# Block sums of the last units and of the first token group moved from GpSimd to VectorE, and a later place for one small product

## The chip, the core and the metric

The kernel runs on one core of a Trainium2 chip. The metric is the time of one execution on the device, in microseconds (us), as the median of several runs. The engines are called as in the profile: PE is TensorE (PEld its weight loads), DVE is VectorE, ACT is ScalarE, POOL is GpSimd, SP is the engine that issues most transfers.

## What is computed

```python
# x: 8 x 3008 x 256, filters: 1505 x 256, all float32 or float64 on input
X = np.fft.rfft(x, axis=1)
Y = X * (filt_r + 1j * filt_i)[None]
y = np.fft.irfft(Y, n=3008, axis=1)            # 8 x 3008 x 256
x2 = y.reshape(24064, 256)
h = x2 @ w_in                                  # 256 -> 2048
g = h - np.tanh(h)
out = g @ w_out                                # 2048 -> 256
```

## The kernel before

**Two halves.** The Fourier part is done as matrix products in steps (`first`, `middle`, `last`) over five batches of sequences called `UNITS` (one, two, two, two, one sequence). The second half, the two large products with the function h - tanh(h) between them, starts as soon as the first batch of sequences has its frequencies back, and the Fourier steps of the later batches are spread between its instructions.

**Token groups and units.** The tokens are cut into 48 groups of up to 512 (the last one has 448). For every group, the 2048 hidden features are cut into four quarters. A group and a quarter together are a *unit* (a word that the code also uses, as `U`, from 0 to 191; it has nothing to do with `UNITS`). The work on a unit goes through three steps: `up` makes h with products on PE, `shrink` turns h into g with arctan and squares on ACT and multiplications on DVE, and `down` multiplies g by `w_out` and accumulates in PSUM. A loop runs `U` from 0 to 193; in each round it interleaves `up(U)`, `shrink(U - 1)` and `down(U - 2)` by hand, as Python generators that are advanced with `next`. Nothing reorders what this loop issues: each engine carries out its own instructions in this order, and waits by semaphores for what it needs. In the last two rounds (`U` of 192 and 193) there is no `up` any more, and a short loop with `k` from 0 to 4 advances `shrink` twice and `down` twice at each `k`.

**Seven products instead of eight.** Both large products are done on blocks of 2 by 2 with seven block products instead of eight (a Strassen scheme). It needs four sums of the blocks of the input beforehand and some sums of the products afterwards. The sums of the input blocks are made by `combine(b, t)`, which issues four subtractions into `t[0]` to `t[3]`; `t[1]` needs `t[0]`, and `t[3]` needs `t[1]`.

- For the first large product the sums are those of the group's tokens. They are made at the end of `last(i)`, into the tile `tu`, from the tile `ut`, 128 x 256 elements each. `up` uses them in its products named x and z (lines L545).
- For the second large product the sums are those of g, and are made at the end of `shrink(U)`, right after `end(0)` (L633, the last multiplication of `shrink`, done in place in the tile `h`), into the tile `t`, 128 x 2 x 256 elements each (128 x 2 x 224 in the last group). `down` uses them: products 1, 2 and 3 read `h` itself, product 5 reads `t[0]`, product 6 `t[1]`, product 7 `t[2]`, product 4 `t[3]` (L680). They are issued in the order (1, 2), (3, 5), (6, 7), (4).

In the kernel before, the four subtractions (L524 to L527) are all on POOL. The one exception is the third of the very last unit, which is on DVE. The weights need the same kind of sums; those are on POOL too (`sums`, L260 to L263), and are made in the first stretch, as the weights come in.

**Around the opening.** The first group's `last(0)` is issued in full before the loop. Then `up(0)` begins: products x and y on `ut`, a copy `s` on ACT, a step of the conversion of late weights on DVE (L204, L205, L207), the sum of h on DVE that reads the bank of y (L571), the product x on `tu`, and then a product `pf` of the next batch's Fourier step, whose PSUM bank is that of y.

**Around the end.** After the last unit's products, `down(191)` adds them up (L693 to L713, on ACT, DVE and POOL), transposes the result on PE (L756), copies it from PSUM (L758, L760) and stores it (L767). Between these, `bounded` decides whether all |h| were below a bound: a comparison of the sums of squares `y_sums` (L781), a minimum over them (L783), a product of that column with a column of ones on PE, `pc` (L785), which adds up the 128 partitions, and a conversion into the integer `count` (L786). The program ends by reading `count`, and goes through a slower general kernel (`general`) if the bound did not hold. With the inputs at hand it holds.

Of the kernel before, what the change touches and what calls it, by code (L numbers as in the profile page):

```python
# [143 lines left out]
def kernel(  # L144
# [162 lines left out]
    def weights_slow(tiles, quarters):  # L307

        jobs = parts_of(quarters)
        began = [begun(tiles, job, True) for job in jobs[:2]]  # L310
        yield
        for k in range(len(jobs)):
            for _ in began[k]:
                yield
            if k + 2 < len(jobs):
                began.append(begun(tiles, jobs[k + 2], True))
            if k % 2:
                sums(quarters[k // 2])
                yield
# [180 lines left out]
    def last(i, z):  # L500


        p, c = groups[i]
        ws_ = widths(p, c)
        n = sum(ws_)
        e2 = e2s.pop(i)
        ut = dn.tile([128, 2, CH * 128], F32, tag="ut", bufs=2, name="ut")
        for h in range(2):
            pu = z("pu", [128, CH * 128])
            for j, w in enumerate(ws_):  # L510
                nc.tensor.matmul(pu[:, j * 128:j * 128 + w], e2[0:w, j, h * 128:(h + 1) * 128],  # L511
                                 s2[0:w, 0:w], start=True, stop=True)
            ACT.copy(ut[:, h, 0:n], pu[:, 0:n])
            if h == 0:
                yield
        w = n // 2
        tu = dn.tile([128, 4, 256], F32, tag="tu", bufs=2, name="tu")
        b = [[ut[:, h, k * w:(k + 1) * w] for k in range(2)] for h in range(2)]
        combine(b, [tu[:, k, 0:w] for k in range(4)])
        uts[i] = (b, tu, w)  # L520
        yield

    def combine(b, t, shared=False):
        G.tensor_sub(t[0], b[0][1], b[0][0])  # L524
        G.tensor_sub(t[1], b[1][1], t[0])  # L525
        (V if shared else G).tensor_sub(t[2], b[1][1], b[0][1])  # L526
        G.tensor_sub(t[3], t[1], b[1][0])  # L527


    hs, gs = {}, {}  # L530
# [76 lines left out]
    def shrink(U):  # L607

        h, w = hs.pop(U)
        ht = {k: h[:, k:k + 2].rearrange("p a b n -> p (a b) n")[:, :, 0:w] for k in (0, 2)}  # L610

        def tiles(tag, bufs):
            return dn.tile([128, 4, 256], F32, tag=tag, bufs=bufs, name=tag)[:, :, 0:w]

        y, sq = {}, {}

        def turn(k):
            y[k] = tiles("y", 2)
            ACT.activation(y[k], ht[k], AF.Arctan, scale=S)  # L619

        def power(k):
            ACT.activation(y[k], y[k], AF.Square,  # L622
                           accum_out=y_sums[:, 2 * U + k // 2:2 * U + k // 2 + 1])

        def times(k):
            V.tensor_mul(ht[k], ht[k], y[k])  # L626

        def square(k):
            sq[k] = tiles("sq", 1)
            ACT.activation(sq[k], y[k], AF.Square, bias=near_b, scale=A)  # L630

        def end(k):
            V.scalar_tensor_tensor(out=ht[k], in0=sq[k], scalar=K, in1=ht[k],  # L633
                                   op0=ALU.add, op1=ALU.mult)


        turn(2)
        power(2)
        yield
        times(2)  # L640
        yield
        square(2)
        turn(0)
        yield
        end(2)
        yield
        power(0)
        times(0)
        square(0)
        yield  # L650
        end(0)
        t = dn.tile([128, 4, 2, 256], F32, tag="t", bufs=2, name="t")
        blocks = [[h[:, 2 * a + k, :, 0:w] for k in range(2)] for a in range(2)]
        combine(blocks, [t[:, k, :, 0:w] for k in range(4)], U + 1 == 4 * len(groups))
        gs[U] = (blocks, t, w)
        yield

# [115 lines left out]
            nc.sync.dma_start(dst, src)  # L773
        del outs[:n]

    def bounded(z):


        small = tr.tile([128, 2 * 4 * len(groups)], F32, tag="a2", bufs=2, name="small")
        least = cst.tile([128, 1], F32, name="least")  # L780
        V.tensor_single_scalar(out=small, in_=y_sums, scalar=float(np.arctan(S * NEAR) ** 2),  # L781
                               op=ALU.is_lt)
        V.tensor_reduce(out=least, in_=small, axis=mybir.AxisListType.X, op=ALU.min)  # L783
        pc = z("pc", [1, 1])
        nc.tensor.matmul(pc, least, ones, start=True, stop=True)  # L785
        V.tensor_copy(count, pc)  # L786

    def general(sb, ps):

# [66 lines left out]
    with tc.tile_pool(name="tr", bufs=2) as tr, tc.manual_schedule():  # L856
        with tc.tile_pool(name="pro", bufs=1) as pro, \
# [136 lines left out]
            for j in range(NK // 2):  # L994
# [7 lines left out]
                for i in range(2):  # L1002
                    k = (2 * j + i) % 4
# [34 lines left out]
        with tc.tile_pool(name="dn", bufs=2) as dn, \  # L1038
# [22 lines left out]
            def filters_d():  # L1061
# [15 lines left out]
                for v, row, m, i, n, src in filter_rows(0, NK):  # L1077
                    G.dma_start(dram(filt_d, ((row * 2 + v) * NK + i) * DM,
                                     [[2 * NK * DM, m], [DM, n], [1, DM]]), src)
                    yield  # L1080

            late, copies = weights_slow(tiles1, range(7, 8)), filters_d()
            total = 4 * len(groups)
            for _ in last(0, z1):
# [2 lines left out]
            for U in range(total + 2):  # L1087
                i, u = divmod(U, 4)
                if U < total:
                    p, c = groups[i]  # L1090
                    if c == 0 and u == 0:
                        units = 4 * len(CHUNKS[p])
                        steps, done = [], 0 if p else EARLY
                        if p + 1 < len(UNITS):
                            n_f = len(chunks_of(UNITS[p + 1], XH))
                            n_m = 2 * NK // (3 - len(UNITS[p + 1]))
                            steps = [0.01 * units + 1.36 * units * (k - done) / (n_f - done)
                                     for k in range(n_f)]
                            lo, hi = 1.6 * units, 5 * units - 17
                            steps += [lo + (hi - lo) * k / n_m for k in range(n_m)]  # L1100
                            ms = None
                    if u == 0 and i + 1 < len(groups) and c + 1 < len(CHUNKS[p]):
                        e2s[i + 1] = load_e2(*groups[i + 1])
                    if u == 2 and i + 1 < len(groups) and c + 1 == len(CHUNKS[p]):
                        assert done == len(steps)
                        e2s[i + 1] = load_e2(*groups[i + 1])
                    if u == 0 and c + 1 == len(CHUNKS[p]) and p + 2 < len(UNITS):
                        fs = first(p + 2, z1)
                        next(fs)
                    if u == 2 and i + 1 < len(groups):  # L1110
                        lasts = last(i + 1, z1)
                sh = shrink(U - 1) if 0 <= U - 1 < total else iter(())
                dw = down(U - 2) if 0 <= U - 2 < total else iter(())

                def d():

                    next(dw, None)

                def e():

                    next(dw, None)

                def s():

                    next(sh, None)

                def t(k):


                    nonlocal ms, done  # L1130
                    quarter[0] = k
                    if k == 2 and stores:
                        store(*stores.pop())
                    store_some(4)
                    if U >= total:
                        return
                    pos = 20 * c + 5 * u + k
                    if u == 3 and k in (0, 2) and i + 1 < len(groups):
                        next(lasts)
                    elif done < len(steps) and steps[done] <= pos:  # L1140
                        if done < n_f:
                            next(fs)
                        else:
                            next(ms)
                        done += 1
                        if done == n_f:
                            ms = middle(p + 1, z1)
                            next(ms)
                    next(late, None)
                    if U > 0 and k in (1, 3):  # L1150
                        next(copies, None)

                if U < total:
                    if U == total - 1:
                        one = tr.tile([128, 128], F32, tag="x", bufs=3, name="one_sb")
                        nc.sync.dma_start(one, one_d)
                        ones = cst.tile([128, 1], F32, name="ones")
                        G.memset(ones, 1.0)
                    up(U, d, e, s, t)
                else:  # L1160
                    for k in range(5):
                        s()
                        s()
                        d()
                        e()
                        t(k)
                        if U == total + 1 and k == 0:
                            bounded(z1)
            for w in stores:
                store(*w)  # L1170
            store_some(len(outs))
# [36 lines left out]
```

## Time and profile before

| | |
|---|---|
| median of 6 runs | 2805.44 us (2802.91 to 2807.14) |
| the profiled execution's own time | 2805.67 us |
| span of its instructions | 2803.9 us |
| busy share of the span: PE, PEld, DVE, ACT, POOL | 97%, 81%, 68%, 67%, 63% |
| mean granted TensorE clock | 0.991 |

The span is the time from the first to the last instruction in the profile. A line of a timeline gives start, length, engine, source line, operation, the tile written and the tiles read, with the shapes, a count of instructions merged into the line and, in brackets, the idle time of that engine before it with what ended it. A line of the chain of work that ended last gives start, length and what. A row of a table by windows gives the window, its length, the busy time of PE, PEld, DVE, ACT and POOL with the count of instructions, the granted TensorE clock as a share, the busy share of the transfer engines, and GB/s.

### The profile page before, as it was taken

What the parts mean: (1) busy time and instruction counts of PE and PEld (TensorE: products, weight loads), DVE (VectorE), ACT (ScalarE), POOL (GpSimd) and SP (SyncE); (2) the same over time, 40 slices, a digit from 0 to 9 for tenths busy, and PEclk for the clock granted to TensorE, in tenths of its full rate; (3) what the DMA queues carried; (4) which work ended last, traced back from release to release, by engine and by line L of the source; (5) the groups of instructions that cost most, each with busy time, mean ns of one, the idle gap of its engine ahead of it and who ended that gap; (6) DMA issues with size and microseconds to landing.
All of it is one profiled execution on the core that took longest, in us unless ns stands there. A gap on an engine that the chain in (4) does not pass through costs nothing.

```text
span 2803.9 us, 36463 instructions
## 1 busy us (share of the span) xinstructions
PE 2718.8 (97%) x12438; PEld 2272.7 (81%) x12438; DVE 1910.4 (68%) x2175; ACT 1886.4 (67%) x2790; POOL 1768.9 (63%) x1407
## 2 busy tenths in 40 slices
PE   4899999999999999999999999999999999999998
PEld 2577778888888888888888888888888888898887
DVE  6755666666776777665677776766676676677776
ACT  2476777666767776666677777666666666666665
POOL 5546887544776777544576777654476667555655
PEclk7999999999999999999999999999999999999999
DMA  9854442322333222223323233112223222111010
GB/s 248 214 185 123 105 126 75 90 83 72 79 78 77 69 72 59 64 78 88 82 70 75 71 81 82 38 45 64 59 67 86 55 58 62 25 20 25 16 22 17
DMA packets 322591, 217.53 MB, mean 78 GB/s; under 512 B 224782, under 2 KB 274746, under 8 KB 322156
## 3 DMA queue, kind: packets, MB, share of 16 engines
q1 hardware_dynamic: 266826, 157.28, 23.6%
q10 hardware_dynamic: 52818, 51.53, 6.0%
q0 software_dynamic: 2752, 6.30, 0.9%
q8 instruction: 100, 1.64, 0.2%
q14 instruction: 95, 0.78, 0.1%
HBM read 138.87 MB, written 79.17 MB: 78 GB/s over the span
## 4 chain that ended last, share of the span: by engine, by line
PE 82%; DVE 6%; ACT 4%; issue 2%; POOL 2%; DMA 2%; SPq 1%; ACTq 0%; DVEq 0%; POOLq 0%
PE o L680 34%; PE x L545 20%; PE z L545 10%; PE y L545 5%; PE pe L411 3%; PE pz L430 3%; PE pu L511 3%; PE pf L351 2%; DVE h L626 2%; ACT y L622 1%; DVE h L596 1%; DMA raw<-in_moe_w_in_dram 1%; ACT y L619 1%; DVE h L633 1%; SPq L773 0%
## 5 line engine op out<-in xcount | busy, mean ns | idle before, releaser
L626 DVE TENSOR_TENSOR h<-h,y 128x1024 f32<-128x1024 f32 (+2 forms) x384 | 575.8, 1500 | 312.3 <-ACT y L622 310.8
L680 PE MATMUL o<-t,wd 128*128 128x256 f32 (+2 forms) x3072 | 776.5, 375 | 1.8 <-POOL t L526 1.3
L680 PEld LDWEIGHTS o<-t,wd 128*128 128x128 f32 x3072 | 580.5, 190 | 93.9 <-issue 22.0
L633 DVE SCALAR_TENSOR_TENSOR h<-sq,h 128x1024 f32<-128x1024 f32 (+2 forms) x384 | 558.8, 1455 | 122.8 <-ACT sq L630 114.8
L524 POOL TENSOR_TENSOR t<-h 128x512 f32<-128x512 f32 (+2 forms) x192 | 240.5, 1253 | 553.0 <-DVE h L633 402.4
L680 PE MATMUL o<-h,wd 128*128 128x256 f32 (+2 forms) x2304 | 582.3, 375 | 4.0 <-DVE h L633 4.0
L545 PE MATMUL x<-tu,wu 128*128 128x256 f32 (+2 forms) x2304 | 582.0, 375 | 4.2 <-POOL tu L525 2.1
L545 PEld LDWEIGHTS x<-tu,wu 128*128 128x128 f32 x2304 | 430.4, 190 | 105.1 <-issue 42.6
L680 PEld LDWEIGHTS o<-h,wd 128*128 128x128 f32 x2304 | 430.1, 190 | 77.4 <-issue 16.0
L630 ACT ACTIVATE sq<-y,near_b 128x1024 f32<-128x1024 f32 (+2 forms) x384 | 435.1, 1133 | 6.5 <-DVE h L633 0.2
L619 ACT ACTIVATE y<-h 128x1024 f32<-128x1024 f32 (+2 forms) x384 | 397.3, 1035 | 14.4 <-ACT e L414 6.4
L622 ACT ACTIVATE y<-y 128x1024 f32<-128x1024 f32 (+2 forms) x384 | 399.9, 1041 | 6.6 <-ACT a L352 0.4
L551 ACT COPY s<-x 128x512 f32<-128x512 f32 (+2 forms) x192 | 110.9, 577 | 327.9 <-PE x L545 309.8
L527 POOL TENSOR_TENSOR t<-t,h 128x512 f32<-128x512 f32 (+2 forms) x192 | 319.0, 1661 | 0.1
L551 ACT COPY u<-x 128x512 f32<-128x512 f32 (+2 forms) x384 | 221.1, 576 | 138.0 <-PE x L545 119.6
L525 POOL TENSOR_TENSOR t<-h,t 128x512 f32<-128x512 f32 (+2 forms) x192 | 246.2, 1282 | 15.1
L526 POOL TENSOR_TENSOR t<-h 128x512 f32<-128x512 f32 (+2 forms) x191 | 245.9, 1287 | 0.0
L446 POOL TENSOR_TENSOR zs<-zs,ft 128x512 f32<-128x512 f32 x112 | 165.2, 1475 | 90.0 <-ACT zs L444 89.9
L447 POOL TENSOR_TENSOR uv<-uv,zs 128x512 f32<-128x512 f32 x112 | 206.8, 1846 | 9.1 <-DVE uv L445 0.5
L545 PE MATMUL x<-ut,wu 128*128 128x256 f32 (+2 forms) x768 | 198.4, 381 | 10.5 <-DVE h L596 8.4
L588 DVE TENSOR_TENSOR h<-z,u 128x512 f32<-128x512 f32 (+2 forms) x192 | 128.8, 671 | 112.1 <-ACT u L551 111.1
L545 PE MATMUL z<-tu,wu 128*128 128x256 f32 (+2 forms) x768 | 194.6, 376 | 0.0
(122 smaller groups left out, 3291.3 us busy)
## 6 DMA issues: line engine op xcount, KB each, us to landing
a<-ct SPq DMA_DIRECT2D x64, 384.0 KB, 3.9
ft<-filt SPq DMA_DIRECT2D x96, 256.0 KB, 4.5
out_dram<-ot SPq DMA_DIRECT2D x1392, 16.0 KB, 1.5
ct<-e ACTq DMA_DIRECT2D x112, 192.0 KB, 2.2
ct<-a ACTq DMA_DIRECT2D x80, 256.0 KB, 2.9
x_sb<-in_x_dram SPq DMA_DIRECT2D x69, 256.0 KB, 2.9
e<-ct SPq DMA_DIRECT2D x33, 512.0 KB, 4.2
fg<-fg SPq DMA_DIRECT2D x40, 392.0 KB, 5.1
```

Of the source, the lines that this page charges most:

```text
L524: G.tensor_sub(t[0], b[0][1], b[0][0])
L525: G.tensor_sub(t[1], b[1][1], t[0])
L526: (V if shared else G).tensor_sub(t[2], b[1][1], b[0][1])
L527: G.tensor_sub(t[3], t[1], b[1][0])
L545: nc.tensor.matmul(bank[:, k], wu[:, q - 1, (2 * u + k) * 128:(2 * u + k + 1) * 128], rhs[q - 1], start=(first and k == 0), stop=True, ski ...
L551: ACT.copy(t, X)
L619: ACT.activation(y[k], ht[k], AF.Arctan, scale=S)
L622: ACT.activation(y[k], y[k], AF.Square, accum_out=y_sums[:, 2 * U + k // 2:2 * U + k // 2 + 1])
L626: V.tensor_mul(ht[k], ht[k], y[k])
L630: ACT.activation(sq[k], y[k], AF.Square, bias=near_b, scale=A)
L633: V.scalar_tensor_tensor(out=ht[k], in0=sq[k], scalar=K, in1=ht[k], op0=ALU.add, op1=ALU.mult)
L680: nc.tensor.matmul(product(q), wd[:, q - 1, (2 * u + k) * 128: (2 * u + k + 1) * 128], rhs[q - 1][:, k], start=(u == 0 and k == 0 and q == ...
```

## The change

`combine` is given the engine for all four subtractions. The sums of `tu` are on DVE for the first group and on POOL for the 47 others. The sums of `t` are on DVE for units 190 and 191 and on POOL for the others. `bounded` becomes a generator with two steps: the comparison and the minimum are issued in the last round at `k` of 0, after the first pair of the last unit's products and before the additions L693 and L694; the product `pc` and the conversion are issued at `k` of 2, after the products (6, 7).

```diff
-        combine(b, [tu[:, k, 0:w] for k in range(4)])
+        combine(b, [tu[:, k, 0:w] for k in range(4)], G if i else V)
...
-    def combine(b, t, shared=False):
-        G.tensor_sub(t[0], b[0][1], b[0][0])
-        G.tensor_sub(t[1], b[1][1], t[0])
-        (V if shared else G).tensor_sub(t[2], b[1][1], b[0][1])
-        G.tensor_sub(t[3], t[1], b[1][0])
+    def combine(b, t, by):
+        by.tensor_sub(t[0], b[0][1], b[0][0])
+        by.tensor_sub(t[1], b[1][1], t[0])
+        by.tensor_sub(t[2], b[1][1], b[0][1])
+        by.tensor_sub(t[3], t[1], b[1][0])
...
-        combine(blocks, [t[:, k, :, 0:w] for k in range(4)], U + 1 == 4 * len(groups))
+        combine(blocks, [t[:, k, :, 0:w] for k in range(4)],
+                G if U + 2 < 4 * len(groups) else V)
...
-    def bounded(z):
+    def bounded():
...
         V.tensor_reduce(out=least, in_=small, axis=mybir.AxisListType.X, op=ALU.min)
-        pc = z("pc", [1, 1])
+        yield
+        pc = z1("pc", [1, 1])
         nc.tensor.matmul(pc, least, ones, start=True, stop=True)
         V.tensor_copy(count, pc)
+        yield
...
+            bound = bounded()
...
                         d()
+                        if U == total + 1 and k in (0, 2):
+                            next(bound)
                         e()
                         t(k)
-                        if U == total + 1 and k == 0:
-                            bounded(z1)
```

As built, the four sums of `tu` of the first group stand on DVE between the conversion passes of earlier weights and L204, that is before L204, L205, L207 and L571. The four sums of unit 190 stand on DVE between L633 of that unit and L604, the last sum of h in unit 191. The four of unit 191 stand behind its last L633; behind them come L781, L783, L694, L700, the conversion to `count` and L705. On PE the order changes only by `pc`, which moves from behind the products (1, 2) to behind (6, 7).

## The prediction

> **What bounds the kernel now.** I read the busy shares first, then the list of who waited for whom on PE, then the chain that ended last, then the instructions around the two edited places.
>
> ```profile
> PE 2718.8 (97%) x12438; PEld 2272.7 (81%) x12438; DVE 1910.4 (68%) x2175; ACT 1886.4 (67%) x2790; POOL 1768.9 (63%) x1407
> ```
>
> The waits, as engine and line, whom it waited for, us in total, times, longest:
>
> ```profile
> PE x L545 <- POOL tu L525: 2.1, 1, 2.1
> PE pc L785 <- DVE least L783: 1.9, 1, 1.9
> ...
> PE o L680 <- POOL t L526: 1.3, 1, 1.3
> ...
> PE o L680 <- POOL t L527: 0.5, 1, 0.5
> ```
>
> PE is the bound, so an edit is worth only the PE idle time it removes, or what it takes off the work after PE's last product. Each of these four waits happens once. The first is in the opening of the first token group, the other three are in the last 30 us. The chain shows how those three follow each other (start, length, what):
>
> ```profile
> 2776.59 1.16 POOL t L524
> ...
> 2777.82 1.86 POOL t L525
> 2779.68 1.94 POOL t L526
> 2781.62 1.95 POOL t L527
> ...
> 2783.61 2.74 PE o L680 x12
> ...
> 2787.68 0.56 DVE least L783
> ...
> 2788.47 4.92 PE o L680 x16
> ```
>
> Unit 190's four sums take 6.97 us on POOL. VectorE works on unit 191 meanwhile, and the two slow each other:
>
> ```profile
> 2775.36 1.08 DVE L633 SCALAR_TENSOR_TENSOR h<-sq,h 128x896 f32<-128x896 f32 x1
> ...
> 2782.67 1.83 DVE L633 SCALAR_TENSOR_TENSOR h<-sq,h 128x896 f32<-128x896 f32 x1
> ...
> 2784.61 0.62 DVE L526 TENSOR_TENSOR t<-h 128x448 f32<-128x448 f32 x1
> ```
>
> The same L633 takes 1.08 us alone and 1.83 beside POOL. One sum costs 0.62 on DVE, 1.14 on POOL undisturbed. After unit 191's first eight product matmuls PE stands still from 2786.34 to 2788.29, because the bound's product is next in its order. Then the clock drops:
>
> ```profile
> 2790.00:2791.00 1.00, 1.00 (x4) 0.93 (x3) 0.02 (x1) 0.35 (x1) 0.00 (x0) 0.50 0.00 0
> ```
>
> The seventh figure, 0.50, is the granted clock. The windows around it (0.84 from 2789 to 2790, 0.96 from 2793 to 2794) put the half clock at about 0.32 + 3 + 0.08 = 3.4 us, costing 1.7 us of PE work.
>
> **Unit 190's sums.** On DVE they stand between L633 (ends 2776.44) and L604, the last sum of h in unit 191. One after another, with 0.03 us before a dependent one, they end at about 2778.9 where POOL ended at 2783.56. PE's 28 product matmuls of unit 190 (0.19 apart) then run without the 1.29 and 0.53 us waits and end near 2782.1. That alone brings nothing: the next product needs unit 191's last L633. Queued behind the sums on DVE are L604, L626, L633, L626, L633. L604 slips from 2776.36 to 2778.8 and ends 2779.4, so ACT's second arctan waits for it (2778.48 before, 2779.45 now). From there: L626 to 2780.4, L633 to 2781.5; the square's ACT pass ends 2781.5 (0.95 + 0.95 + 0.19); L626 to 2782.6, L633 to 2783.8, all at the undisturbed 1.07 to 1.08 us since POOL is silent. PE starts unit 191 at 2783.83 instead of 2784.56: **0.7 us gained**. Beyond those five nothing waits for the sums. No DMA is moved, nor any queue passed.
>
> **Unit 191's sums and the bound.** The sums follow L633 on DVE and end at 2784.4, 2785.0, 2785.6 and 2786.2. The products that read them come 1.5 us (first) and 3.0 us (second and third) after PE's start, that is from 2785.3 and 2786.9, so PE does not wait. The comparison and the reduction (0.53 + 0.56) stand behind the sums on DVE and end near 2787.3, under PE's products, so they cost nothing; without that cover they would cost 1.1. L694 and L700 wait behind them, but nobody needs those before L707. The bound's product now follows the third pair of products at 2788.4 and finds its input ready. Removed: from the end of eight matmuls at 0.19 (2786.07) to the restart at 2788.41, **2.3 us**. New on the path: the bound's two matmuls and the conversion to `count` (0.15) stand before L705 on DVE: **0.2 us lost**.
>
> **The clock.** In the profiled run the 16 matmuls from 2788.41 took 4.98 us; at 0.19 each they take 3.2: **1.8 us**. Whether this goes depends on idle time. The 1.95 us gap was followed by half clock; those of 1.29 and 0.53 were not, nor was PE's longest wait between 200 and 600 us (3.3, for POOL's `uv` near 245: the clock reads 1.00 from 240 to 270). So length alone does not decide; where the gap falls does too. The new gap before unit 191, 2782.06 to 2783.83, is 1.8 us. I take it as mostly not enough, as it is shorter than the two (1.95, and 2.08 in the opening) that did bring half clock. The Trainium skill ("TensorE: Matmul & The Clock Gate", section "Why this matters for your kernels") asks for no PE-idle gaps over about 3 us; this trace drops the clock after 1.95, so the measurement decides. By the page neither gap would drop it, and this term would be nothing.
>
> Tail: 0.7 + 2.3 + 1.8 - 0.2 = **4.6 us**; L705 comes at 2788.8 instead of 2793.42. What follows (L706, L707, L713, the transposes, the two stores) keeps its lengths. If half clock hits unit 191 in the new kernel, 1.7 comes back: 2.9.
>
> **The first group's sums.** They gain nothing, though their wait is the longest of the four.
>
> ```profile
> 122.34 0.79 POOL L261 TENSOR_TENSOR wd<-wd 128x256 f32<-128x256 f32 x1
> ...
> 124.40 0.69 DVE L571 TENSOR_TENSOR h<-y,s 128x512 f32<-128x512 f32 x1 [0.98 <-ACT s L551]
> ...
> 126.29 1.14 PE L545 MATMUL x<-tu,wu 128*128 128x256 f32 x4 [2.08 <-POOL tu L525]
> ...
> 127.25 1.88 PE L351 MATMUL pf<-x_sb,wf_sb 128*128 128x512 f32 x2
> ```
>
> On POOL they stand behind four sums of `wd` (to 124.69). On DVE they start when the first copy of `ut` ends, 122.2 (the transfers they also wait for are those PE's first matmul of the group waited for, which started at 122.22), in front of three conversion passes (L204, L205, L207; 0.42 each) and of L571. The matmul on `tu` can start at 124.05, 2.2 us earlier. But the next one in PE's order, `pf`, writes the bank that L571 reads, and L571 now stands behind seven instructions. Beside POOL's `wd` sums each DVE sum waits for a POOL one: the rows show a blocked DVE instruction ending 0.28 (L205, L207) after its POOL neighbour, and a blocked POOL one of this size 0.6 after its own. Alternating gives 122.6, 123.5, 124.4 and 125.3 for the four, 126.4 after the conversions, L571 to 127.04, `pf` at 127.28 against 127.25: **0.0**. If POOL never got in the way (0.42 each from 122.2), `pf` would be held only to about 126.7: 0.6 gained. If each DVE sum cost a whole POOL instruction (0.8) and its full 0.42, the four end at 127.0 and `pf` comes at 129.0: 1.7 lost. I take 0, nearest to the L205 and L207 rows, which stand beside the very same POOL sums. The Trainium skill ("SBUF — State Buffer", section "Who interferes with whom") speaks against this edit: a VectorE instruction with two SBUF inputs and a GpSimd one reading SBUF exclude each other for the whole instruction. L571, with one input in PSUM, kept its 0.69 beside POOL, as the page says. With the full 0.42 after each block the page would put `pf` some 0.5 us later than my sum.
>
> The opening also ran at half clock for 3.4 us (0.73 from 125 to 130, 0.93 from 130 to 135) behind a 2.08 us idle; the new idle is 125.2 to 127.3, as long. So this stays, unless it falls differently on the clock's accounting: then up to 1.4 us go (133.48 now, 132.05 with the two `pf`, `z` and copies at full clock).
>
> **Sum.** The profiled execution took 2805.67 us, a span of 2803.9 and 1.8 around it, 0.2 above the median 2805.44. 2805.67 - 4.6 = 2801.0. I keep 2801.0 for the median; 0.2 is less than the terms are known to. Of this kernel, a measurement can tell about 0.2% from no change, 5.6 us: below 2799.8 is faster, above 2811.1 slower.
>
> **Rivals.**
> (a) As forecast, and the opening's half clock goes or POOL's `wd` sums hardly block: 0.6 to 2.0 more (both), 2799.0 to 2800.4, half of it past the bound. For it: half clock depends on where the idle falls, and this idle moves. Against: idle as long as before.
> (b) Half clock comes after the new gap before unit 191, or `pf` is held by whole POOL instructions: 1.7 each, 2802.7, both 2804.4.
> (c) Slower: the sums do not run at 0.62 on DVE. Unit 190's four delay unit 191's last L633 fourfold, and the sixth product needs three more. With s for one sum (over 1.0, so that the sums and not PE set the pace), L705 comes at 2783.8 + 4(s - 0.62) + 3s + 2.1, which passes 2793.42 at s = 1.43; at POOL's disturbed 1.95 the end is 3.6 us later, 2809.3. Against it: the 0.62 row is the same shape and operands, even started just before a POOL sum.
> (d) The edits do nothing: excluded, the order of VectorE's and PE's instructions does change as told.
>
> **Numbers.** Forecast 0.52, (a) 0.30, (b) 0.13, (c) 0.05. Half of (a), 0.15, lies past the bound for faster, and a quarter of the forecast, 0.13, since the six times before spread over 4.2 us and its middle is only 1.2 from the bound: 0.28. Slower by more than 0.2% needs 7(s - 1.43) above 5.4, s above 2.2: 0.03. Range 2799.0 to 2804.2: the low end takes in (a), the high end nearly all of (b).
>
> **What would show it.** PE's wait for `least` and both waits for `t` in the last units gone; L526 at 0.62 on DVE eight times over; L633 at 1.08 throughout the tail; a PE gap of about 1.8 us before unit 191's first product; from that product to L705 some 4.9 us, where it was 8.9. In the opening, the matmul on `tu` near 124.1 and `pf` still near 127.3. Wrong if `pf` moves by over a microsecond, if L604 delays unit 191 past 2784.6, or if the bound's product still waits.

## The result, and the profile after

The changed kernel takes 2800.47 us in the median of 17 runs, beside 2805.97 us for the kernel before in 37. The ratio is 0.998, with a 95% interval of 0.9974 to 0.9987: about 5.5 us less, 0.20%, with an interval that leaves out 1. The forecast was 2801.0 us, with a range of 2799.0 to 2804.2. Two later measurements of the same kernel gave 0.9982 and 0.9983. The ratios here and below are those on record; they are estimates of their own, not the quotient of the two medians, and differ from it by up to 0.0003.

The two profiled executions are closer together: 2805.67 and 2802.76 us, 2.9 us apart. From unit 190's last L633 to `pu` they differ by 4.5 us. But the first copy of `ut` ends 1.3 us later in the changed one (122.17 and 123.44); this end lies anywhere from 121.2 to 123.9 in the fourteen profiles of this document. Single executions scatter by more than the terms of the sum, so the terms are read below from distances within a trace.

The page of the changed kernel's profile (span, then busy us, share and instructions) shows eleven instructions fewer on POOL and eleven more on DVE:

```profile
span 2800.9 us, 36459 instructions
...
PE 2717.0 (97%) x12438; PEld 2271.3 (81%) x12438; DVE 1914.9 (68%) x2186; ACT 1886.9 (67%) x2790; POOL 1755.4 (63%) x1396
```

In the list of PE's waits (us in total, times, longest) of the changed kernel, `tu` on POOL, `least` and both waits for `t` are gone. Two others have come or grown:

```profile
PE o L682 <- DVE h L633: 5.8, 9, 1.8
...
PE pf L351 <- DVE h L571: 1.7, 1, 1.7
```

The first is the new gap before unit 191's first product (1.81 us, forecast 1.8). The second is the opening's idle, moved from the product on `tu` to `pf`.

The chain of work that ended last (start, length, what) now runs through DVE in the tail, where it ran through POOL. Source lines moved by two at this place; L705 is now L707.

```profile
2777.64 0.64 DVE t L524
...
2778.30 0.62 DVE t L525
2778.92 0.54 DVE t L526
2779.46 0.53 DVE t L527
2779.99 0.53 DVE h L604
...
2783.89 1.10 DVE h L633
...
2785.04 4.81 PE o L682 x24
...
2790.15 0.31 DVE pu L707
```

Unit 190's four sums take 2.36 us, from 2777.64 to 2780.00, instead of 6.97, L604 waits behind them as forecast, and 24 of unit 191's products run in one piece.

### The profile page after: what moved, and what is told of

Read it like the earlier page. It is cut to its first block, busy times and chain, and to the rows that moved or that the text cites. A ratio compares the mean times of both kernels' runs of the same rounds, so it can differ in the third digit from the quotient of the medians.

```text
span 2800.9 us, 36459 instructions
## 1 busy us (share of the span) xinstructions
PE 2717.0 (97%) x12438; PEld 2271.3 (81%) x12438; DVE 1914.9 (68%) x2186; ACT 1886.9 (67%) x2790; POOL 1755.4 (63%) x1396
## 4 chain that ended last, share of the span: by engine, by line
PE 82%; DVE 6%; ACT 5%; DMA 3%; issue 2%; POOL 2%; ACTq 0%; SPq 0%; DVEq 0%; POOLq 0%
PE o L682 34%; PE x L545 20%; PE z L545 10%; PE y L545 5%; PE pe L411 3%; PE pz L430 3%; PE pu L511 3%; DVE h L626 2%; PE pf L351 2%; ACT y L622 1%; ACT y L619 1%; DVE h L596 1%; DMA raw<-in_moe_w_in_dram 1%; DVE h L633 1%; ACT sq L630 0%
## 5 line engine op out<-in xcount | busy, mean ns | idle before, releaser
L626 DVE TENSOR_TENSOR h<-h,y 128x1024 f32<-128x1024 f32 (+2 forms) x384 | 576.2, 1501 | 311.9 <-ACT y L622 310.8
L633 DVE SCALAR_TENSOR_TENSOR h<-sq,h 128x1024 f32<-128x1024 f32 (+2 forms) x384 | 558.9, 1455 | 122.4 <-ACT sq L630 114.0
```

## The experiments

For every kernel I read four distances from its trace: from the end of the first copy of `ut` to `pf` and to the first product of `down`; from unit 190's last L633 to unit 191's first product and to `pu` (L705 before, L707 after); and the granted clock. "Before" in a row is the kernel before on the same chip.

**Each part alone.** The parts are the three pieces of the change: the sums of `tu`, the sums of `t`, and the place of `bounded`. The cuttings are shortened. In the first run `combine` for `t` and the place of `bounded` are as before; in the second `tu` and `bounded`; in the third both `combine` calls; in the fourth only `tu`.

```diff
 e2, e3, e4:  combine(b, [tu ...], G)                    # first group's sums on POOL
 e1, e3:  combine(blocks, [t ...], as before: POOL, third of unit 191 on V)
 e1, e2:  e(); t(k); if k == 0: next(bound); next(bound)    # bound at its old place
```

> Only the first group's sums of tu are on VectorE; units 190 and 191 and the bound's product are as before. Theory A (the opening gives nothing, all of the gain is made in the tail): the median stays within 0.7 us of before (ratio 1.0000 +- 0.0003), and pf (L351) starts about as long after the end of the first copy of ut as before (5.1 us). Theory B (the opening has a share, since the changed kernel's profile shows pf only 4.7 us after that copy, and no half clock behind it): 1 to 2 us faster (ratio 0.9993 to 0.9996), with PE's wait before pf under 1.8 us and full clock from there on. In the tail PE's waits for t and for least, and the 1.95 us gap, must stand as before.

> Only the eight sums of units 190 and 191 are on VectorE; the bound's comparison, minimum and product follow the first pair of products as before. Theory A (sums and bound are separate terms, 0.7 us for the sums): unit 191's first product starts about 7.4 us after unit 190's last L633 ends (8.1 before); the product pc still holds PE, behind four sums, L694, L781 and L783 on VectorE, for about 2 us, so the gain is 0.6 us and half clock can still follow (ratio about 0.9998). Rival C (the sums were the whole cause, the bound's wait is only there because VectorE was slowed by POOL): PE's wait for least shrinks below 0.5 us and the gain is 3 us or more (0.9989).

> Only the bound is moved: comparison and minimum after the first pair of unit 191's products, pc after (6, 7). All sums are as before, on POOL but for the third of unit 191. Theory A: unit 191's first product starts 8.1 us after unit 190's last L633 as before, PE's wait for least is gone, L705 comes 2.1 us earlier after that product if the clock stays full or half in both, and 3.9 earlier where the half clock goes with the gap: 2.1 to 3.9 us faster (ratio 0.9986 to 0.9993). Rival C: POOL's sums of unit 191 hold PE instead (t[1] and t[3] on POOL come 2.9 and 4.1 us after L633), and the gain is under 1.5 us.

> The whole change except the first group: tu is on POOL for all groups. Theory A (the opening gives nothing): as fast as the changed kernel, 4.5 to 5.5 us faster than before (ratio 0.998). Theory B (the opening has a share of 1 to 2 us): 3.5 to 4.5 us faster (0.9984 to 0.9988), and in the profile PE waits 2.1 us for POOL's tu again. In both the tail must look like the changed kernel's, L705 about 12.5 us after the end of unit 190's last L633.

| kernel | `ut` to `pf`, to first `down` | L633 to unit 191, to `pu` | median, before beside it | ratio, interval |
|---|---|---|---|---|
| before | 5.09, 29.30 | 8.11, 16.98 | | |
| changed | 4.72, 27.44 | 7.43, 12.47 | 2800.47, 2805.97 | 0.998 (0.9974 to 0.9987) |
| e1, opening | 4.72, 27.43 | 8.11, 16.98 | 2806.96, 2807.31 | 0.9998 (0.9989 to 1.0007) |
| e2, sums | 5.50, 29.38 | 7.44, 14.60 | 2806.00, 2807.31 | 0.9992 (0.9983 to 1.0001) |
| e3, bound | 5.55, 29.59 | 8.12, 13.16 | 2804.01, 2807.31 | 0.9985 (0.9976 to 0.9994) |
| e4, sums and bound | 5.16, 27.84 | 7.44, 12.48 | 2802.77, 2807.31 | 0.9984 (0.9975 to 0.9993) |

The medians alone would not separate the parts; the distances do, to a few hundredths of a microsecond. The sums bring 0.67 us (8.11 to 7.44) and leave PE's wait for the bound standing, so rival C (the sums were everything) falls. The timeline of e2 shows that wait, and DVE at its undisturbed speed under it:

```profile
2786.22 0.35 DVE L783 TENSOR_SCALAR small<-y_sums 128x384 f32<-128x384 f32 x1
2786.61 0.55 DVE L785 TENSOR_REDUCE least<-small 128x1 f32<-128x384 f32 x1
2787.31 0.19 PE L788 MATMUL pc<-ones,least 128*1 128x1 f32 x2 [1.93 <-DVE least L785]
...
2788.67 2.81 PE L682 MATMUL o<-t,wd 128*128 128x224 f32 x14
```

The last 14 products take 2.81 us here. In the kernel before they took 4.49 under half clock, behind a gap 0.02 us longer. Moving the bound brings 2.1 us at full clock: `pu` comes 7.16 us after unit 191's first product in e2 and 5.04 in e4, which differ in nothing else in the tail. In e3 POOL's sums of unit 191 are ready in time, so rival C falls there too.

e1 gives half to each of its theories: `pf` at 4.72 and no half clock in the opening, as theory B expected, but a median within 0.4 us of before, as theory A did; half clock came at 246.8 us instead. e4's ratio of 0.9984 lies on the border between its two theories and decides nothing.

**Only unit 190's sums.** e4, with unit 191's sums as before (POOL, the third on VectorE).

> tu on POOL for all groups, the bound moved, unit 190's four sums on VectorE, unit 191's sums as before (POOL, the third on VectorE). Theory A (unit 191's sums are ready in time on either engine; the 0.7 us come from unit 190's): L705 12.5 to 12.8 us after unit 190's last L633, as in e4, and the same median within 0.5 us (ratio 0.9984). Rival C (the sums of the last unit matter, since nothing is left to hide them): PE waits 0.5 to 1.5 us for t of unit 191, L705 at 13.0 to 14.0.

Unit 191 starts 7.43 us after L633 and `pu` comes at 12.47 us, within 0.01 of e4 (2801.86 us, ratio 0.9982, 0.9973 to 0.9992). The four sums of unit 191 on VectorE are worth nothing here; all of the 0.67 us comes from unit 190's.

**A busy POOL.** The changed kernel with six more subtractions on POOL, whose results are not used.

```diff
+        if U + 2 == 4 * len(groups):
+            scr = dn.tile([128, 4, 256], F32, tag="tu", bufs=2, name="scr")
+            for k in range(6):
+                G.tensor_sub(scr[:, 2 * (k % 2):2 * (k % 2) + 2, 0:w], blocks[0][1], blocks[0][0])
```

> The changed kernel with six subtractions that nobody reads put on POOL beside unit 190's sums and unit 191's multiplications; they read SBUF only. It prices the silent POOL that the sum for the tail rests on. Theory A (VectorE instructions with two SBUF inputs take turns with POOL): the sums take 0.95 to 1.8 us instead of 0.62, L626 and L633 1.8 to 2.0 instead of 1.08, L604, with one input in PSUM, stays at 0.61; unit 191's first product 11 to 13.5 us after unit 190's last L633 (7.4 in the changed kernel), so that a tail with the sums on VectorE beside a busy POOL is slower than the tail before (8.1). Rival (POOL is the one that waits): 7.4 to 8.0 us, the sums at 0.62.

The timeline of this kernel:

```profile
2776.46 0.63 DVE L524 TENSOR_TENSOR t<-h 128x448 f32<-128x448 f32 x1
...
2777.12 1.44 DVE L525 TENSOR_TENSOR t<-h,t 128x448 f32<-128x448 f32 x1
...
2781.43 0.61 DVE L604 TENSOR_TENSOR h<-z,u 128x448 f32<-128x448 f32 x1
...
2783.55 1.84 DVE L633 SCALAR_TENSOR_TENSOR h<-sq,h 128x896 f32<-128x896 f32 x1
...
2788.58 4.10 PE L686 MATMUL o<-h,wd 128*128 128x224 f32 x10 [6.00 <-DVE h L633]
```

Sums with two SBUF inputs wait for POOL (1.44, then 1.55 and 1.55; the first, started ahead of POOL, keeps 0.63); L604, with one input in PSUM, does not. L626 and L633 took 1.49, 1.84 and 2.02 us as long as POOL worked, less than expected for the first, and the last L633, after POOL was done, 1.09. Unit 191 starts 12.16 us after L633, inside the expected 11 to 13.5, and `pu` comes 2.3 us later than in the kernel before (half clock fell into both tails). So the sums are cheap on VectorE only because POOL is silent in the tail. This is the mechanism of the prediction's slower rival; the time is that of a single execution, 2807.66 us.

**PE kept busy in the gap.** The kernel before, with work on PE that the result does not need.

```diff
+        fill = z("fill", [128, 2, 128])
+        for _ in range(4):
+            nc.tensor.matmul(fill, wf1[:, 0], wf1, start=True, stop=True)
         pc = z("pc", [1, 1])
```

> The kernel before, with four matmuls of 128x256 that nobody reads put on PE ahead of pc, so that PE works for about 1.7 us of the 1.95 us gap. It adds work that the result does not need. Theory A (the half clock in the tail comes from the gap): never half clock in the tail, L705 7.1 to 7.4 us after unit 191's first product instead of 8.9, so 0.8 to 1.7 us faster on the median, depending on how often the gap brings half clock (ratio 0.9994 to 0.9997). Rival D (the half clock falls there whatever PE does, or the matmuls delay pc): no gain or up to 0.5 us slower.

2804.14 us beside 2805.46 (ratio 0.9995, 0.9986 to 1.0004): inconclusive. In its profile half clock came earlier, from 2786.6 to 2790.0, behind the two waits for POOL's `t` (1.29 and 0.53) that the filler does not cover, and `pu` 8.0 us after unit 191's first product. Theory A's "never half clock" is wrong: those two waits together can bring it (here both lie whole in the 3.41 us ahead of it; the last section says why that matters).

**Other openings.** All three are the changed kernel otherwise. In e7 and e8 the first step of the late conversion is left out at the first unit's first quarter, so that every later step comes a quarter later; in e7 and e9 only `t[0]` and `t[1]` of `tu` are on VectorE; in e9 the step follows L571 within the same quarter. The cuttings are shortened, and one line is in words.

```diff
 e7, e8:  -   next(late, None)
          +   if U or k: next(late, None)
 e7, e9:  t[0], t[1] on V and t[2], t[3] on POOL, for the first group
 e9:      -   t(0)                                   # before L571
          +   if U: t(0)
              d(); shrinks(0)
              V.tensor_add(h[:, 0, :, 0:w], Y, s1)   # L571
          +   if not U: t(0)
```

> The changed kernel with another opening: for the first group only t[0] and t[1] of tu are on VectorE, t[2] and t[3] on POOL, and the first step of the late conversion (L204, L205, L207) comes one quarter later, so that L571 stands right behind t[1]. If what stands in front of L571 holds pf, as the prediction's sum for the opening says, pf starts 3.1 to 3.4 us after the first copy of ut (4.7 in the changed kernel, 5.1 before), and the first down product 1.3 to 1.7 us earlier than in the changed kernel: 1.0 to 1.7 us faster than the changed kernel (ratio to before about 0.9975). If the opening's gains are given back later (half clock that comes behind the wait for uv near 246 us whenever it does not come in the opening), the stretch from the copy of ut to unit 190's last L633 stays within 0.5 us of 2654.2 and the median within 0.7 us of the changed kernel's.

> The changed kernel with the first step of the late conversion one quarter later and all four sums of tu on VectorE. L571 follows the fourth sum: pf 3.9 to 4.1 us after the first copy of ut, 0.7 us earlier than in the changed kernel, where it stands behind three conversions. On the median 0.5 to 0.8 us faster than the changed kernel, or the same if the opening's gains are given back near 246 us.

> The changed kernel with another opening: t[0] and t[1] of the first group's tu on VectorE, t[2] and t[3] on POOL, and L571 ahead of L204, L205 and L207; the late conversion keeps its quarter. If e7 lost its gain only because the conversion came a quarter later and fell on unit 1's L597, this one keeps it: pf 2.9 us after the first copy of ut and the first down product at 25.6 to 26.3 us (27.4 in the changed kernel), 1 to 1.8 us faster than the changed kernel (ratio to it 0.9994 to 0.9996), unless the half clock near 246 us takes it back. If ACT's and VectorE's chain through unit 0 sets the first down product whatever PE does: 27.0 to 27.5, and no gain.

| kernel | `ut` to `pf`, to first `down` | median, changed kernel beside it | ratio to before, interval |
|---|---|---|---|
| changed | 4.72, 27.44 | | |
| e7 | 2.90, 27.45 | 2800.77, 2801.22 | 0.9986 (0.9977 to 0.9995) |
| e8 | 3.71, 28.08 | 2802.36, 2801.22 | 0.9986 (0.9977 to 0.9995) |
| e9 | 2.90, 25.68 | 2798.40, 2802.07 | 0.9973 (0.9962 to 0.9983) |

Expected of the yardsticks:

> The changed kernel once more, as the yardstick for the two runs with another opening beside it. Theory A (tail 4.5 us, opening 0 to 0.5 us): 4 to 6 us faster than before (ratio 0.998 to 0.9985), L705 12.5 us after unit 190's last L633.

> The changed kernel, as the yardstick for the other opening beside it: 4 to 6 us faster than before (ratio 0.998 to 0.9985).

They gave 0.9982 (0.9973 to 0.9991) and 0.9983 (0.9974 to 0.9992), with `pu` 12.47 us after L633 in both.

`pf` came earlier in all three, at the 2.9 us expected in e9 and 0.2 us earlier than expected in e7 and e8: what stands in front of L571 does hold it. By the first `down` product the gain was gone in e7, and e8 was 0.6 us later than the changed kernel. The timeline of e7 shows where: the late conversion's last step, a quarter later, now stands on DVE ahead of L597, unit 1's copy of h (L596 before), and PE waits 1.93 us for that, 0.46 in the changed kernel.

```profile
142.47 0.83 DVE L230 SCALAR_TENSOR_TENSOR wd<-ft,pt 128x256 f32<-128x256 f32 x3
143.21 0.68 DVE L597 COPY h<-x 128x512 f32<-128x512 f32 x1
...
143.95 1.13 PE L546 MATMUL x<-ut,wu 128*128 128x256 f32 x4 [1.93 <-DVE h L597]
```

e9 leaves the quarter as it was and keeps the 1.76 us:

```profile
124.96 0.69 DVE L573 TENSOR_TENSOR h<-y,s 128x512 f32<-128x512 f32 x1 [0.83 <-PE y L546]
...
125.70 1.13 PE L351 MATMUL pf<-x_sb,wf_sb 128*128 128x512 f32 x2
```

L573 is L571 of the other kernels; `pf` now follows the product on `tu` with no gap. e9 has the lowest median, 3.7 us under the changed kernel beside it. The intervals of their ratios to before overlap, and of the 3.7 us the trace explains 1.76; its profiled run also had no half clock near 246 us, which the changed kernel's three profiles had (3.41 to 6.83 us of it). Whether that belongs to this opening or to this execution is not shown.

**Where half clock falls in the opening.** The rows of the table by windows (window, length, busy times, clock, transfer share, GB/s) around the wait for `uv` near 246 us, of the kernel before and then of the changed kernel:

```profile
243.00:253.00 10.00, 6.68 (x27) 4.79 (x26) 3.49 (x4) 5.94 (x9) 7.58 (x6) 1.00 1.01 246
```

```profile
243.00:253.00 10.00, 6.68 (x21) 4.53 (x20) 3.16 (x4) 5.19 (x8) 7.14 (x5) 0.83 1.04 245
```

The eight profiles with the first two sums of `tu` on VectorE have none in the opening, and seven of them have it near 246. Of the six with `tu` on POOL, five have it in the opening, and three near 246. From the copy of `ut` to unit 190's last L633, the kernel before took 2654.28 us and the changed one 2654.16 in the profiled runs: the 1.9 us by which the first `down` product came earlier (29.30 to 27.44) had been given back. Most of the 1.9 us was half clock and not the sums: e4, with `tu` on POOL but no half clock in the opening, has that product at 27.84. Over the profiles of this kind the mean is 2655.1 with `tu` on POOL (before, e2 to e6) and 2654.2 in the changed order (changed, its two repeats, e1, e10), but the two sets overlap (2654.1 to 2656.6, and 2653.6 to 2655.4). So the opening's gain is some 0.4 us by e4's distance, 0.9 by these means, and may be nothing by e1's ratio; the runs do not settle it.

## Why the prediction was right, point by point

- **Unit 190's sums.** Forecast 0.7 us, measured 0.67. The order on DVE, the slip of L604 and the wait of ACT's second arctan (0.82 us) are as told. The gap before unit 191 was forecast at 1.8 and is 1.81.
- **Unit 191's sums and the bound.** Forecast 2.3 - 0.2 = 2.1, measured 2.12 (7.16 to 5.04). That unit 191's sums on VectorE would cost nothing was right; e5 shows that they bring nothing either.
- **The clock.** Forecast 1.8, measured 1.70 between two profiles, the one before (8.86) and e2 (7.16). But e2 had no half clock behind a 1.93 us gap, so the kernel before loses this term in some executions only; the forecast took it as always there, and this part of its sum rested on luck, on what the one profiled execution happened to have. The clock records show what decides: the clock changes only at the edges of windows of 3.41 us, and PE's idle time within one window counts (last section). In the kernel before the 1.95 us lay whole within one window of 3.41 us (2786.26 to 2789.67), while in e2 a window's edge at 2785.70 cut the 1.93 us into 0.32 and 1.61. If the edges fall evenly over executions, a gap of 1.95 us escapes the edge in (3.41 - 1.95) / 3.41 = 43% of them, and the term is worth about 0.7 us on the average instead of 1.8: an estimate, and a low one, since e6 shows that the two waits ahead can bring half clock too. That the new gap is mostly too short held: none of the eight profiles with a gap of 1.81 or 1.82 us and no POOL work beside it shows half clock in the tail's products.
- **The tail's sum.** 4.6 forecast, 4.51 measured between the two profiles (16.98 to 12.47). With the clock's term at its estimated average it is about 3.5.
- **The opening.** Forecast 0.0 with `pf` 5.1 us after the copy of `ut`; it came at 4.72. The alternation with POOL was right: sums forecast to end 0.4, 1.3, 2.2 and 3.1 us after the copy ended at 0.46, 1.34, 2.20 and 3.06. Of the missing 0.4, 0.2 was a weight load that I put behind the wait, and the rest L571's end, 4.68 for 4.87. The full 0.42 after a block, which I took from the page's wording and weighed as 0.5 us later, is not what happened: the three blocked sums ended 0.27 to 0.29 us after their POOL neighbours. The statement that the opening's half clock stays was wrong for its place (no profile of the changed order shows it there) and nearly right in sum, since it mostly came back near 246 us.
- **Rivals.** (a), half clock leaving the opening, happened in the profiles but was paid again later. (b) did not happen in any profile of the changed order with POOL silent. (c) did not happen, and e10 shows what a busy POOL would have cost. The first measurement gives 5.5 us (interval 3.6 to 7.3), the tail 4.5 as profiled and about 3.5 by the estimate above. e4 and e5, with `tu` on POOL throughout, came out 4.5 and 5.0 us faster by their ratios (intervals from 2.0 to 7.6). So the size of the gain beyond the 2.8 us of the sums and the bound (0.67 + 2.12) is shown only within such intervals; how it divides between half clock, opening and chance stays open.

## What to carry to other kernels

At the end of this kernel an engine that had been a helper became the critical path: work that was spread over two engines to balance them went faster on the one that is quicker at it, with the other silent, and a side result is best asked for only when its inputs have long been ready. Taking one wait away in a filled order pays only as far as the next instruction that stands behind the same queue: here PE's product was freed 2.2 us earlier and the one after it by 0.4, until the sum that it needed was put ahead of the work that nobody waited for. Where medians scatter by several us, distances between marked instructions in the traces separate terms of half a microsecond.

## What the runs showed of the hardware

- From 100 us to the last products, half clock came in pieces of 3.41 us or 6.83, on a grid that runs through the whole execution: in the clock record of the kernel before, the starts at 127.28 and 2789.67 us lie 780.0 times 3.4133 apart. The Trainium skill ("TensorE: Matmul & The Clock Gate", Part 1) speaks of a free-running window of this length; the runs agree. What they add is that much less than a window of idle is enough: PE idle of 1.93 to 1.95 us brought it in two profiles of three, of 2.07 to 2.36 in five of six, while the wait of 3.3 us near 246 did not bring it in four profiles of fourteen.
- The idle time within one window of that grid sorts these cases. Add up PE's idle time in each window of the fourteen records (those that end after 100 us and before the last 9 us): the 22 windows at full clock with 2.04 us or more (up to 3.41) were all followed by half clock, and none of those with 1.81 us or less was. Of the eight from 1.82 to 1.96 us, three were (1.82 in e6, 1.95 before and in e1). A gap that the edge of a window cuts counts as two: the four waits of 3.3 us without half clock were cut into parts of at most 1.94 us (1.85 and 1.47 in the kernel before), the opening's 2.14 us in e4 into 1.96 and 0.18. In the changed kernel's second repeat the new gap of 1.81 us lay whole within one window, and no half clock followed.
- With POOL busy, PE's idle of 6.0 us was followed by a piece of half clock of 6.83 us (e10), and unit 191's first ten products took 4.10 us where they take 2.16.
